# A written-out order of 6,000 steps, replaced by another, with ten steps removed, in an RWKV-7 plus SwiGLU kernel

## The chip, the cores and the metric

The program runs on one core of a Trainium2 chip. A core has a matrix engine (TensorE; its matmuls are called PE in the profile, its weight loads PEld), a vector engine (VectorE, DVE), an activation engine (ScalarE, ACT), a general engine (GpSimd, POOL) and a sync engine (SyncE, SP) that only issues DMA transfers. Matmuls read SBUF and write PSUM; the other engines move results from PSUM to SBUF. Each engine takes its instructions in the order in which the program lists them and waits on semaphores for the other engines.

The metric is the device time of one execution in microseconds, less is better. The median of several executions is compared.

## The reference

Inputs have batch 4, heads 8, sequence 768, head size 40 for the recurrent part; the feed-forward part has 3072 tokens of width 320 and 1536 hidden units. Everything is float32 on the chip; the feed-forward weights arrive as 64-bit floats. Cut to what is computed:

```python
for t in range(S):                        # per batch and head
    y[:, :, t] = einsum('bhd,bhde->bhe', r_t, state)
    Sa = einsum('bhde,bhe->bhd', state, a_t)
    state = state * w_t - outer(Sa, b_t) + outer(v_t, k_t)

x = y.transpose(0, 2, 1, 3).reshape(B * S, H * D)
xn = x / sqrt(mean(x * x) + 1e-6) * rms_g
g = xn @ w_gate
out = (g * sigmoid(g) * (xn @ w_val)) @ w_out
```

The state that stands after the last token is not an output, and the state before the first token is zero.

## The kernel before

**Chunks.** The 768 tokens are cut into 24 chunks of 32. For each chunk there are three stages. `front(c)` loads w, a, k, b and v, transposes them (helper `turned`), forms Gram matrices of k, b and a in levels of 1, 2, 4, 8 and 16 tokens with the decays between them, and writes the 32x32 triangular matrices `LT` to DRAM (`sB`) and back in another layout (`M`). `inverse(c)` inverts these matrices with some 60 small DVE operations and takes the result to DRAM (`sY`) and back into `LT`. `main(c)` multiplies the carried state `ST` by the decayed a (`aP`, kind "state"), adds the local part and solves with `LT` (kind "lower"), puts the solution into `VU`, updates the state (kind "update"), forms the scores with r, sums the levels into `y`, normalises, and leaves transposed rows in `xg`. Chunks 0 to 4 (`BLOCKED`) solve in two blocks, with two solves and a correction between them.

**Feed-forward.** `feed(g)` takes the rows of two chunks (one in the first and the last group; 13 groups) through the 12 slices of the hidden units: kinds "h64" and "hh" for gate and value, Silu on ACT, a product on DVE (`hT`), and "out" into the PSUM tile `po`. `narrow(f, h)` turns the 64-bit weights into 32-bit floats, 24 times five DVE operations and two on ACT, and it all falls into the lead of the program, since group 0 needs all 12 slices.

**The order.** Nothing is issued while these functions run. Each operation becomes a `Piece` with its engine, its needs and its issue function: 6003 in all, of which PE has 1093 (a piece is a group of matmuls, 2 to 64 instructions), DVE 2746, ACT 1092, SP 548 and POOL 524. `Plan.issue` (line 341) then issues them in the order that the text `ORDER` (line 33) writes out: each word is an offset, counted from the first piece that has not yet been issued. So ORDER sets the order on every engine and every DMA queue. `PAIRS` (line 238) gives for each use of a PSUM room (497) which of three PSUM pairs it takes. Semaphores come from the data: an order can't change a result, only the waits.

**What sets when a buffer is free.** `wan` (w and a, later r of a chunk pair) has one buffer, `M` and `Yi` one, `VU`, `LT`, `K`, `ST` and `KN` two.

**Lines that the change touches.** In `front`, line 779 on: per level `K1` is K decayed once more (DVE, and an ACT copy of the other half), `ends` (lines 789 to 798) make the next A, which at level 16 is `aP`, line 799 makes the next product of decays, `Tl[2 * l]`; line 808 on transposes the last K into `KN[32]`. In `main`, line 861: `Sdec`, the decayed state; line 881: the update and the new state.

- `aP` is read in `main` by the kind "state" alone, which runs for c > 0.
- `KN[32]` is read by the kind "update" alone.
- `Tl[32]` is read by `Sdec` alone.

The loop that calls all this goes over c from -2 to 23: `main(c)`, `feed` where a group ends, then `front(c + 2)` and `inverse(c + 2)`.

Of the kernel before, what the change touches and what calls it, by code (L numbers as in the profile page):

```python
# [16 lines left out]
P = 128  # L17
# [16 lines left out]
76 70 3 72 73 2 4 204 697 196 46 36 5 6 25 0 0 58 59 60 199 40 0 53 55 56 340 51 52 40 60 61 67 0 41 73 72 62 363  # L34
190 82 83 199 193 200 46 362 188 383 0 41 0 0 4 45 17 14 16 15 81 371 379 0 0 0 17 18 59 69 47 177 0 18 13 386 364
23 176 60 385 365 679 89 0 355 356 65 357 68 189 177 67 77 80 93 0 80 361 103 4 0 1 21 25 89 74 99 113 101 22 373
374 356 2 90 4 357 0 0 10 366 367 660 169 661 53 3 56 55 84 344 86 361 345 377 62 66 378 350 351 362 71 96 95 363
352 107 370 371 70 364 74 73 67 15 45 44 46 372 353 68 82 81 69 78 98 83 93 92 79 97 89 90 354 63 94 100 101 109 105
80 110 104 112 111 114 171 91 103 653 373 115 355 113 178 179 180 9 160 117 119 118 20 365 356 374 185 379 106 102
22 375 116 389 182 183 186 192 380 381 376 397 196 191 193 197 195 181 208 187 188 382 120 387 407 406 54 293 198  # L40
386 121 194 204 388 122 123 209 124 207 125 167 202 126 127 189 128 203 129 292 130 206 190 131 383 199 215 132 213
133 214 134 384 135 205 219 136 24 409 408 0 173 162 394 214 133 381 424 425 213 134 196 206 208 222 135 207 217 136
395 396 397 137 218 228 138 139 140 227 229 160 226 386 141 142 290 644 216 648 172 143 144 145 146 148 655 398 406
219 387 388 399 389 400 147 231 390 220 401 391 232 230 445 233 407 392 408 409 646 426 427 410 180 428 411 221 293
412 149 444 236 237 429 275 291 645 434 197 647 653 14 663 292 238 239 430 240 433 435 446 276 241 242 243 431 447
153 448 244 223 245 104 246 432 247 225 152 150 668 669 151 277 248 436 437 278 279 438 439 249 449 250 251 450 252
280 281 451 454 455 453 253 456 457 458 254 452 255 440 256 441 257 258 475 476 459 442 259 460 496 285 282 284 495
260 443 486 261 461 262 485 477 283 234 235 294 286 295 654 662 652 650 263 484 478 479 462 264 212 224 265 487 463
287 266 268 269 497 480 498 298 267 306 305 315 303 307 316 299 300 499 767 670 304 302 301 504 505 507 506 481 488
500 308 311 270 0 311 500 677 308 488 273 312 650 489 14 839 823 0 231 46 2 1 0 195 18 22 196 23 186 24 25 469 470  # L50
472 368 197 26 187 251 540 207 371 370 212 198 231 369 381 473 383 375 385 388 376 474 526 525 213 214 27 28 399 386
215 475 476 430 230 398 29 387 410 216 384 217 397 30 396 477 479 481 478 31 480 395 406 530 533 538 539 536 537 250
241 232 218 377 392 378 233 393 394 234 379 484 32 485 252 235 242 240 239 380 389 391 529 527 409 405 408 390 400
407 253 254 364 543 0 0 370 371 203 210 204 368 378 222 384 379 387 389 390 388 393 391 394 392 385 211 205 229 381
212 223 382 380 369 213 455 459 458 383 228 214 224 466 469 516 457 456 215 465 460 462 463 461 468 216 470 225 249
471 464 467 472 398 399 400 401 402 476 403 517 474 0 2 385 403 404 472 476 405 406 407 477 408 409 0 0 395 327 328
396 329 330 331 332 311 312 418 164 428 431 430 429 435 333 334 391 143 142 436 335 336 337 338 339 340 341 545 544
365 415 248 342 343 345 346 344 347 348 349 442 417 446 437 366 397 546 549 548 547 441 529 443 166 167 448 447 438
445 444 439 452 440 456 458 350 351 454 453 457 455 530 449 465 451 414 459 468 464 463 450 146 460 461 469 471 472
482 480 462 467 532 533 434 147 148 470 466 483 481 486 487 168 663 473 149 674 150 151 425 478 534 476 169 152 485  # L60
477 484 474 490 424 535 536 537 170 171 538 539 479 172 173 540 531 475 541 491 492 493 494 495 496 497 498 499 500
369 370 542 676 664 675 681 662 670 665 667 677 671 673 666 543 550 678 551 501 502 503 504 505 506 507 508 509 672
398 399 400 510 680 401 686 511 512 513 687 402 554 555 556 783 185 174 176 514 515 516 517 518 519 520 175 558 177
178 557 523 522 521 524 562 560 563 179 180 564 559 561 181 182 566 565 568 183 184 573 569 567 570 571 525 528 403
527 575 572 574 576 784 577 578 786 186 187 188 579 842 843 841 526 854 580 488 489 682 840 685 844 683 785 189 744
787 788 789 669 697 684 851 839 790 404 581 702 405 407 696 406 190 191 688 192 689 690 847 582 695 700 712 710 713
698 699 724 733 701 791 795 709 711 793 792 583 794 691 798 584 585 721 692 707 693 708 552 694 703 720 732 799 706
719 717 195 194 193 196 197 718 722 723 553 704 714 715 725 729 726 731 705 730 727 716 802 807 728 804 803 736 806
810 813 815 816 805 811 809 198 199 200 0 0 4 6 806 810 815 816 812 584 817 732 733 735 738 820 818 821 5 739 737
736 743 744 745 746 747 1 0 0 737 738 745 746 4 0 0 701 702 773 703 704 628 799 801 797 798 806 617 705 706 774 707  # L70
708 770 775 709 776 777 808 810 952 802 953 811 807 710 814 1078 1075 1082 1073 809 823 1083 711 1085 1072 1074 828
0 0 1087 5 813 0 3 5 0 0 811 4 707 708 822 709 807 808 46 47 48 53 821 816 710 817 819 711 830 52 54 49 712 820 713
0 829 840 0 781 783 782 664 5 665 0 665 790 761 666 762 776 667 670 669 778 777 763 764 773 792 791 789 787 46 0 47
42 43 770 769 44 49 788 783 48 50 45 89 797 663 666 779 781 794 90 780 684 790 791 799 800 798 0 0 0 642 652 710 594
701 384 386 387 1 576 0 10 17 6 785 0 1 650 0 380 700 8 10 573 697 927 638 922 9 2 4 712 11 5 0 698 571 12 14 779
780 782 15 591 592 796 0 792 794 702 700 703 701 568 778 0 0 0 767 768 781 365 769 770 772 773 771 367 366 695 696
697 698 699 700 701 702 703 704 706 705 708 709 710 711 712 713 714 715 716 717 718 719 720 721 722 723 724 725 726
727 728 729 730 0 1 773 782 706 730 602 603 604 605 894 783 370 731 732 733 734 735 736 367 606 372 371 368 373 797
800 799 737 738 739 786 792 740 741 787 788 918 919 905 742 743 744 904 2 789 791 745 369 374 790 793 796 746 798
794 805 795 806 801 912 747 802 748 895 803 804 807 808 809 810 1109 811 914 812 749 1098 1097 0 1102 913 747 748  # L80
912 1093 1104 926 931 749 751 750 752 0 542 546 547 570 558 0 5 0 5 314 550 551 553 554 315 9 0 565 5 6 0 0 552 543
544 561 545 576 558 559 562 564 546 376 378 377 555 557 560 575 574 556 569 570 572 227 573 571 13 595 582 7 12 9 8
10 14 15 566 567 577 578 579 730 568 394 580 585 0 0 0 212 214 213 1 215 379 649 388 389 417 572 570 571 574 575 573
576 418 419 420 524 567 565 421 2 4 580 581 363 585 582 583 587 584 589 586 3 647 648 8 5 591 588 590 593 594 712
505 703 650 592 595 596 597 598 599 600 601 602 364 651 655 653 708 707 704 718 654 7 0 0 0 0 641 647 1 566 592 593
594 595 596 597 598 599 600 601 648 651 657 567 602 656 603 604 605 652 658 606 662 664 665 607 2 7 8 653 4 654 608
655 661 699 504 659 609 660 610 666 611 667 612 9 10 663 668 669 671 670 613 672 614 673 674 615 675 616 676 3 5 617
618 0 671 682 962 487 702 704 6 706 8 613 614 842 0 7 400 698 702 711 610 611 612 613 614 704 615 616 700 617 619
712 705 706 710 715 725 716 618 620 714 959 713 960 958 969 727 723 717 726 707 728 724 9 721 736 708 967 970 838
492 722 709 718 738 737 720 733 719 732 0 6 0 0 0 4 615 617 616 618 728 628 629 723 724 734 735 745 742 743 744 747  # L90
749 729 733 737 748 540 739 746 725 678 688 689 822 395 396 398 397 0 733 731 828 830 747 682 955 829 394 815 816
# [314 lines left out]
def kernel(  # L406
# [41 lines left out]
    N = 8  # L448
# [256 lines left out]
    def front(c):  # L705
# [59 lines left out]
        for j, l in list(enumerate(LEVELS))[2:]:  # L765
# [11 lines left out]

            t = Tl[l].rearrange("p n (g x) -> p n g x", x=2)
            K1 = K_.next()
            if G == 1:  # L780
                tt(K1[:, :, :, 0:16], K[:, :, :, 0:16], t[:, :, None, :, 1].to_broadcast((P, NI, 2, 16)), MUL)
            else:
                for x in range(2):
# [316 lines left out]
```

## Time and profile before

| what | value |
|---|---|
| executions | 1035.87, 1037.38, 1040.97 us |
| median of the three | 1037.38 us |
| the profiled execution, its own time | 1039.87 us |
| its span, first to last instruction | 1038.0 us |
| mean granted TensorE clock in it | 0.952 of full |
| first feed matmul starts, last one ends | 182.8, 1032.8 us |
| feed groups 1 to 10, one each | 69 to 79 us |

The profile gives, for one execution, the busy time of each engine, the same in 40 equal slices, the clock that TensorE was granted (in tenths), the chain of waits that ended last, and groups of equal instructions with their total and mean duration. Busy time on PE is a union over overlapping matmuls: a matmul's own duration (some 200 ns for the small ones) is longer than its share of PE, since many small ones run side by side on parts of the array. Where a PE step is priced below, the time from its first matmul's start to the next step's first start is taken, from the timeline.

### The profile page before, as it was taken

How to read it: one execution, taken by the hardware profiler on the slowest of the kernel's cores; microseconds unless marked ns; L12 is line 12 of the kernel's file. 1: busy time of each engine (PE TensorE's matmuls, PEld its weight loads, DVE VectorE, ACT ScalarE, POOL GpSimd, SP SyncE). 2: the span in 40 equal slices, each digit the busy share in tenths (PEclk: the TensorE clock that was granted, in tenths of full speed). 3: DMA queues.
4: the chain of work that ended last, by engine and by line, in shares of the span. 5: the costliest groups of instructions: out<-in, count | busy, mean ns of one | idle time of the engine just before them, and what ended most of it. 6: DMA issues, size and time to landing. Idle time of an engine off the chain costs nothing.

```text
span 1038.0 us, 55525 instructions
## 1 busy us (share of the span) xinstructions
PE 934.5 (90%) x24592; PEld 760.3 (73%) x24592; DVE 790.2 (76%) x2747; ACT 498.4 (48%) x1113; POOL 306.6 (30%) x530
## 2 busy tenths in 40 slices
PE   2546767999999999999999999999999999999998
PEld 2445756877777878777778777777787787788777
DVE  8989978867869778868778679678697787777531
ACT  5566556453454464464454544534534635436131
POOL 9523234221432242233331324123232413400000
PEclk9957667899999999999999999999999999999999
DMA  7675443222242242232231232232322422420100
GB/s 159 145 173 120 99 93 82 56 63 54 43 84 38 47 95 43 60 79 42 59 84 28 62 75 55 55 68 36 76 45 55 81 41 65 75 44 8 43 7 21
DMA packets 147056, 68.89 MB, mean 66 GB/s; under 512 B 121088, under 2 KB 136384, under 8 KB 146816
## 3 DMA queue, kind: packets, MB, share of 16 engines
q1 hardware_dynamic: 128448, 42.37, 18.4%
q0 software_dynamic: 16192, 22.64, 11.8%
q8 instruction: 193, 3.16, 1.3%
q10 hardware_dynamic: 2176, 0.33, 0.2%
q14 instruction: 47, 0.39, 0.1%
HBM read 55.05 MB, written 10.22 MB: 63 GB/s over the span
## 4 chain that ended last, share of the span: by engine, by line
PE 70%; DVE 9%; DMA 7%; SPq 4%; issue 4%; ACT 2%; DVEq 0%; ACTq 0%
PE ps L532 50%; PE po L532 14%; PE ps L535 6%; SPq L529 4%; DVE Yi L486 2%; DMA LT<-sY 2%; DMA sY<-Yi 2%; DVE tmp L486 1%; DMA sB<-LT 1%; DVE LT L486 1%; DVE wf L486 1%; DMA M<-sB 1%; DVE K L486 1%; DVE y L486 1%; DVE As L486 0%
## 5 line engine op out<-in xcount | busy, mean ns | idle before, releaser
L532 PE MATMUL ps<-xg,wf 128*128 128x256 f32 (+3 forms) x1872 | 361.1, 375 | 1.1 <-DVE hT L486 0.9
L532 PEld LDWEIGHTS ps<-xg,wf 128*128 128x128 f32 (+1 forms) x1872 | 267.7, 190 | 49.1 <-issue 13.2
L532 PE MATMUL po<-wf,hT 128*128 128x320 f32 x576 | 179.7, 446 | 1.1 <-issue 1.1
L486 DVE TENSOR_TENSOR hT<-ps,sg 128x256 f32<-128x256 f32 (+1 forms) x156 | 59.8, 398 | 94.1 <-PE ps L532 56.0
L532 PEld LDWEIGHTS po<-wf,hT 128*128 128x128 f32 x576 | 102.9, 189 | 38.6 <-issue 4.0
L486 DVE TENSOR_TENSOR tmp<-Yi,M 128x24 f32<-128x24 f32 (+21 forms) x512 | 106.6, 208 | 17.4 <-DMA M<-sB 4.5
L486 DVE TENSOR_TENSOR Yi<-Yi,tmp 128x24 f32<-128x24 f32 (+21 forms) x512 | 106.8, 209 | 10.6
L509 ACT ACTIVATE sg<-ps 128x256 f32<-128x256 f32 (+1 forms) x156 | 54.0, 369 | 109.8 <-PE ps L532 106.8
L529 POOL DMA_DIRECT2D VU<-in_v_dram x92 | 53.9, 587 | 155.4 <-PE ps L532 134.4
L486 DVE TENSOR_TENSOR K<-K,T 128x512 f32<-128x512 f32 (+1 forms) x192 | 93.2, 501 | 4.4 <-PE ps L532 1.9
L519 POOL TENSOR_TENSOR ss<-ss,mhalf 128x1 f32<-128x1 f32 x24 | 14.3, 596 | 255.1 <-DVE ss L486 255.0
L532 PE MATMUL ps<-Ab,K 64*60 64x56 f32 (+2 forms) x4608 | 76.3, 220 | 12.7 <-issue 2.4
L532 PEld LDWEIGHTS ps<-Ab,K 64*60 64x60 f32 (+2 forms) x4608 | 69.3, 132 | 22.4 <-issue 10.1
L513 ACT COPY KN<-ps 128x640 f32<-128x640 f32 x96 | 65.8, 692 | 38.8 <-DVE LT L486 24.4
L529 POOL DMA_DIRECT2D kbn<-in_k_dram x92 | 54.1, 589 | 98.5 <-PE ps L532 98.5
L486 DVE TENSOR_TENSOR As<-ps,msi 128x256 f32<-128x256 f32 (+1 forms) x168 | 70.9, 453 | 15.5 <-PE ps L532 10.9
L529 POOL DMA_DIRECT2D kbn<-in_b_dram x92 | 54.1, 589 | 82.9 <-PE ps L532 81.3
L532 PEld LDWEIGHTS ps<-As,KN 128*40 128x40 f32 x3072 | 67.3, 128 | 11.6 <-issue 4.1
L532 PE MATMUL ps<-As,KN 128*40 128x32 f32 x3072 | 72.6, 208 | 2.4 <-DVE As L486 1.2
L513 ACT COPY K<-K 128x512 f32<-128x512 f32 x96 | 61.0, 636 | 27.1 <-PE ps L532 11.8
L486 DVE SCALAR_TENSOR_TENSOR Yi<-M,Yi 128x31 f32<-128x31 f32 (+6 forms) x228 | 44.5, 243 | 36.7 <-DMA M<-sB 20.0
L529 POOL DMA_DIRECT2D wn<-in_w_dram x92 | 51.8, 565 | 43.7 <-DVE KN L486 43.5
(131 smaller groups left out, 1503.4 us busy)
## 6 DMA issues: line engine op xcount, KB each, us to landing
M<-sB SPq DMA_DIRECT2D x96, 128.0 KB, 3.0
wan<-in_r_dram SPq DMA_DIRECT2D x24, 160.0 KB, 4.0
kbn<-in_k_dram POOLq DMA_DIRECT2D x92, 40.0 KB, 2.6
kbn<-in_b_dram POOLq DMA_DIRECT2D x92, 40.0 KB, 2.9
VU<-in_v_dram POOLq DMA_DIRECT2D x92, 40.0 KB, 2.7
wan<-in_w_dram POOLq DMA_DIRECT2D x46, 80.0 KB, 3.2
wan<-in_a_dram POOLq DMA_DIRECT2D x46, 80.0 KB, 2.8
wn<-in_w_dram POOLq DMA_DIRECT2D x92, 40.0 KB, 2.8
```

The lines of the kernel that those rows point to most:

```text
L486: plan.add("DVE", time + more + each * size(o), 0.087, lambda at: [fn(at(o), *m(at))], [o], aps(*args))
L509: scalar(o, [a], lambda at: nc.scalar.activation(at(o), at(a), f, **kw), aps(acc), 0.1 if f in (AF.Square, AF.Relu) else 0.0)
L513: scalar(o, [a], lambda at: nc.scalar.copy(at(o), at(a)), extra=more)
L519: plan.add("POOL", 0.5, 0.06, lambda at: nc.gpsimd.tensor_tensor(o, a, b, op), [o], [a, b])
L529: plan.add(by, 0.6 if by == "POOL" else 0.45, 0.0, lambda at: queue.dma_start(out=o, in_=i), [o], [i], load=load, since=since)
L532: return o, lhsT, rhs, lambda at: nc.tensor.matmul(at(o), lhsT, rhs, start=start, stop=stop, skip_group_check=True), 4
L535: return o, i, ident, lambda at: nc.tensor.transpose(at(o), i, ident), 2
```

## The change

Two things are done. ORDER and PAIRS are written anew: another order of the same steps, less ten. And ten steps are gone: for the last chunk (23) the decayed K at level 16 (a DVE operation and an ACT copy), `Tl[32]`, the transposes into `KN[32]` and their copy, `Sdec` and the update; for the first chunk (0) `aP` (a DVE operation and an ACT copy) and `Tl[32]`. The number of steps falls from 6003 to 5993 and that of PSUM rooms from 497 to 495. No constant, buffer or instruction of the remaining steps is changed. All lines of ORDER and PAIRS are replaced; a few are shown.

```diff
--- before.py
+++ after.py
 ORDER = """
-76 70 3 72 73 2 4 204 697 196 46 36 5 6 25 0 0 58 59 60 199 40 0 53 55 56 340 51 52 40 60 61 67 0 41 73 72 62 363
-190 82 83 199 193 200 46 362 188 383 0 41 0 0 4 45 17 14 16 15 81 371 379 0 0 0 17 18 59 69 47 177 0 18 13 386 364
...
+86 83 81 0 0 53 0 1 44 0 64 0 65 76 196 199 45 0 0 38 0 52 0 57 0 5 0 0 51 0 36 0 43 47 57 69 353 354 355 70 72 76
+78 362 0 173 186 8 75 89 371 57 81 58 56 189 94 59 82 0 0 90 58 360 352 353 2 370 371 103 0 181 19 184 90 3 113 378
...
 """
 
 PAIRS = """
-01201210121021200021102212200010110200100201020112101002120121012212012212110202010010102012120120012002120020000011
...
+01201022101021010120102221102210012100101011200212202001210220201002022222210211010102211001002121002012011110021101
...
 """
...
@@ -776,14 +776,18 @@
             copy(z["KN"][l].rearrange("p (n o e) -> p n o e", n=N, o=2), gr.rearrange("p o n t -> p n o t")[:, :, :, 16:16 + D])
 
             t = Tl[l].rearrange("p n (g x) -> p n g x", x=2)
-            K1 = K_.next()
-            if G == 1:
-                tt(K1[:, :, :, 0:16], K[:, :, :, 0:16], t[:, :, None, :, 1].to_broadcast((P, NI, 2, 16)), MUL)
-            else:
-                for x in range(2):
-                    tt(side(K1[:, :, x], l, 0), side(K[:, :, x], l, 0), t[:, :, :, 1, None].to_broadcast((P, NI, G, l)), MUL)
-            kn_ = lambda k: k.rearrange("p n x (g h l) -> p (n x) g h l", h=2, l=l)[:, :, :, 1]
-            copy(kn_(K1), kn_(K))
+            if G > 1 or c + 1 < NCH:
+                K1 = K_.next()
+                if G == 1:
+                    tt(K1[:, :, :, 0:16], K[:, :, :, 0:16], t[:, :, None, :, 1].to_broadcast((P, NI, 2, 16)), MUL)
+                else:
+                    for x in range(2):
+                        tt(side(K1[:, :, x], l, 0), side(K[:, :, x], l, 0), t[:, :, :, 1, None].to_broadcast((P, NI, G, l)), MUL)
+                kn_ = lambda k: k.rearrange("p n x (g h l) -> p (n x) g h l", h=2, l=l)[:, :, :, 1]
+                copy(kn_(K1), kn_(K))
+            if l == 16 and c == 0:
+                K = K1
+                break
             if l == 16:
                 A1, A0 = aP_.next(), A[:, :, 0:C]
                 ends = [(side(A1, l, 1), side(A1, l, 0), side(A0, l, 1), side(A0, l, 0), t[:, :, :, 0, None].to_broadcast((P, NI, G, l)))]
@@ -796,7 +800,8 @@
             for r1, l1, r0, l0, w_ in ends:
                 tt(r1, r0, w_, MUL)
                 copy(l1, l0)
-            tt(Tl[2 * l], t[:, :, :, 0], t[:, :, :, 1], MUL)
+            if G > 1 or c + 1 < NCH:
+                tt(Tl[2 * l], t[:, :, :, 0], t[:, :, :, 1], MUL)
             K, A = K1, A1
 
         sB = sB_.next()
@@ -805,9 +810,10 @@
         z["M"] = M = M_.next()
         for m in range(4):
             dma(M[m * BH:(m + 1) * BH].rearrange("p b x -> p (b x)")[:, 0:C * C], sB, "M")
-        z["KN"][32] = KN_[32].next()
-        copy(z["KN"][32].rearrange("p (n o e) -> p n o e", n=N, o=2),
-             turned(K.rearrange("p (n i) x s -> p n (i x s)", i=2), ins=TOP, outs=P)[:, :, :, 0:D])
+        if c + 1 < NCH:
+            z["KN"][32] = KN_[32].next()
+            copy(z["KN"][32].rearrange("p (n o e) -> p n o e", n=N, o=2),
+                 turned(K.rearrange("p (n i) x s -> p n (i x s)", i=2), ins=TOP, outs=P)[:, :, :, 0:D])
         z["aP"] = A
 
     def inverse(c):
@@ -859,7 +865,7 @@
         pe("lower", [mm(X[other(i, n), o, col(n % 4)], LT[own(i, n), o * N + slot(n)], VU[own(i, n), n, o, 0:D], c == 0 and n % 4 == 0, n % 4 == 3)
                     for n, i, o in by_q])
         Sdec = Sdec_.next()
-        if c > 0:
+        if 0 < c < NCH - 1:
             tt(Sdec, ST.rearrange("p n i d -> p (n i) d")[:, :, 0:D], z["T"][32].to_broadcast((P, NI, D)), MUL)
         Xs = Xs_.next()
         scale(Xs, X[:, :, 0:4 * D], -1.0)
@@ -878,14 +884,15 @@
         for i, q in each_iq:
             copy(VU[other(i, 4 * q), 4 * q:4 * q + 4, :, 0:D].rearrange("p n o d -> p o n d"),
                              U[other(i, 4 * q), :, 0:4 * D].rearrange("p o (n d) -> p o n d", n=4), more=0.09)
-        up = plan.room()
-        pe("update", [mm(up[part(o), i, col(slot(n))], kn(z, 32, i, n, o), VU[half(i), n, o, 0:D]) for n, i, o in each])
-        if c == 0:
-            copy(ST_.next()[:, :, :, 0:D].rearrange("p n i d -> p i n d"), up[:, :, 0:N * D].rearrange("p i (n d) -> p i n d", n=N))
-        elif c + 1 < NCH:
-            tt(ST_.next()[:, :, :, 0:D].rearrange("p n i d -> p i n d"),
-               up[:, :, 0:N * D].rearrange("p i (n d) -> p i n d", n=N),
-               Sdec.rearrange("p (n i) d -> p i n d", n=N), ADD)
+        if c + 1 < NCH:
+            up = plan.room()
+            pe("update", [mm(up[part(o), i, col(slot(n))], kn(z, 32, i, n, o), VU[half(i), n, o, 0:D]) for n, i, o in each])
+            if c == 0:
+                copy(ST_.next()[:, :, :, 0:D].rearrange("p n i d -> p i n d"), up[:, :, 0:N * D].rearrange("p i (n d) -> p i n d", n=N))
+            else:
+                tt(ST_.next()[:, :, :, 0:D].rearrange("p n i d -> p i n d"),
+                   up[:, :, 0:N * D].rearrange("p i (n d) -> p i n d", n=N),
+                   Sdec.rearrange("p (n i) d -> p i n d", n=N), ADD)
         if c % 2 == 0:
             tk = slice(c * C, (c + 2) * C)
             t = rn.next()
```

## What the change does to the time: a forecast

> **What bounds the kernel now.** I read the page's first two parts, then a table of five stretches, then the chain of waits, then groups kept apart by shape, for the prices.
>
> ```profile
> span 1038.0 us, 55525 instructions
> PE 934.5 (90%) x24592; PEld 760.3 (73%) x24592; DVE 790.2 (76%) x2747; ACT 498.4 (48%) x1113; POOL 306.6 (30%) x530
> ...
> PE   2546767999999999999999999999999999999998
> DVE  8989978867869778868778679678697787777531
> PEclk9957667899999999999999999999999999999999
> ```
>
> PE is full from the eighth slice (26 us each) to the end. Before that DVE is the full engine and the granted clock is low. The stretches say it in microseconds:
>
> ```profile
> core 0: us, PE busy (x) PEld busy (x) DVE busy (x) ACT busy (x) POOL busy (x), PEclk, DMA share, GB/s
> 0.00:47.00 47.00, 19.06 (x588) 17.18 (x592) 43.13 (x123) 24.76 (x46) 34.87 (x68) 1.00 0.69 152
> 47.00:187.00 140.00, 92.00 (x3493) 82.33 (x3483) 119.47 (x354) 86.97 (x176) 46.09 (x77) 0.65 0.50 114
> 187.00:222.00 35.00, 33.94 (x952) 29.07 (x948) 27.55 (x104) 15.51 (x37) 8.58 (x15) 1.00 0.29 58
> 222.00:1008.00 786.00, 763.74 (x19354) 610.75 (x19341) 596.47 (x2155) 365.05 (x835) 216.54 (x369) 1.00 0.27 55
> ```
>
> Up to 47 us DVE is busy 92% (43.13 of 47). From 47 to 187 it is busy 85%, at a clock of 0.65, so 20.5 us of it are idle. From 222 us PE is busy 97% at full clock. So the time is a DVE-bound lead of some 190 us plus the PE work left then. The chain agrees: 70% PE, 9% DVE, 7% DMA. A sum over the timeline (first feed matmul starts at 182.8 us, the last ends at 1032.8) leaves 5 us at the end, for the copy and store of the last rows.
>
> **Part 1: the removed work.** These groups give the prices:
>
> ```profile
> L535 PE MATMUL ps<-ident,K 40*128 40x40 f32 x384 | 17.4, 239 | 1.8 <-DVE y L486 0.9 <-DVE hT L486 0.8
> L532 PE MATMUL ps<-VU,KN 64*40 64x40 f32 x1536 | 22.7, 212 | 4.7 <-issue 4.4 <-ACT VU L513 0.3
> ...
> L486 DVE TENSOR_TENSOR K<-K,T 128x512 f32<-128x512 f32 x48 | 32.9, 686 | 1.8 <-ACT K L513 0.8 <-ACT T L513 0.7
> L486 DVE TENSOR_TENSOR Sdec<-ST,T 128x640 f32<-128x640 f32 x23 | 18.8, 818 | 0.2
> ...
> L486 DVE TENSOR_TENSOR aP<-Ab,T 128x256 f32<-128x256 f32 x24 | 10.0, 417 | 0.0
> ...
> L486 DVE TENSOR_TENSOR T<-T 128x16 f32<-128x16 f32 x24 | 4.0, 168 | 0.1
> ```
>
> Last chunk. The 16 transposes of K run at 969 us, where PE is full; from their start to the next step's takes 0.52 us at the median, so -0.5. The 64-instruction update runs at 1032.90, behind the last feed matmul, beside the copy and store that end the program: 0 (0.83 us if it stood earlier). DVE loses 0.69 (K), 0.17 (T) and 0.82 (Sdec), ACT the copies K (0.62) and KN (0.70). All lie at 956 to 971 us beside a full PE, and DVE waits on PE in that stretch: 0; without that cover 1.7.
>
> First chunk. DVE loses aP 0.42 and T 0.17, in the lead, where DVE is the bound: -0.6. ACT's copy of aP (0.39 at 21 us) hides behind DVE: 0. **Part 1: -1.1.**
>
> **Part 2: the new order.** Each word of ORDER is a place counted from the first step not yet issued, so both lists can be read off as steps and compared. They are near neighbours. Of the 1091 PE steps in both, half move by at most one place and nine in ten by at most 4; DVE, ACT and SP at most 7, 6 and 7; POOL, which issues most loads, 16. Every DMA is still issued, on the queue it had. One is moved past others: the first half of chunk 0's r load now stands on SP ahead of the four sB stores of chunk 0, which wait behind it until chunk 1's w and a are transposed (28.4 us; sB went at 29.0). Price 0.45 (one issue) to 4.0 (its landing); I take it inside the lead's bounds below.
>
> **Changes of array shape.** In the timeline from 225 us a full 128-row feed step of four matmuls takes 0.863 us, start to start, before another of its shape, and 0.957 before a step of another shape; for the output steps it is 1.076 and 1.170. So a change costs 0.094. From the first feed step on the old list has 480 changes, the new 477: **-0.3.**
>
> **Work ahead.** For each PE step I add the DVE work listed before it (each operation by the median of its group's start-to-start spacing, or its duration) and the PE work from it to the end (median spacing by kind). The largest sum over all steps is what the two engines need between them: 965.1 before, 963.4 after, so -1.7. Of this, 0.8 is the update that costs nothing and 1.1 is part 1, so the order adds **+0.2.** At the first feed step the sum falls from 964.2 to 961.6: 155.1 us of DVE work stand ahead of it before, 151.5 after, while the PE work done by then falls only from 64.1 to 61.8.
>
> **The lead's idle time.** These 73 us between 965 and 1038 are idle time that no list shows. The largest piece is DVE's in the lead:
>
> ```profile
> 130.00:156.00 26.00, 16.45 (x676) 14.68 (x680) 19.56 (x66) 14.74 (x30) 8.29 (x14) 0.68 0.42 93
> 156.00:182.00 26.00, 19.02 (x819) 17.06 (x815) 20.52 (x53) 16.02 (x37) 11.81 (x20) 0.76 0.39 80
> ```
>
> 11.9 us in these two slices (52 less 40.1). There chunks 2 and 3 pass through their inverse, and its result goes from SBUF to DRAM (sY) and back (LT) before PE can solve. The DVE work put between the inverse's last operation and that solve grows from 9.0 to 13.4 us for chunk 2 and from 10.0 to 12.7 for chunk 3; the way took 10.5 and 11.6 in the trace. So 7.1 us more of DVE work fills stretches in which it idled. Bounds: 0 (the idle comes back one wait later) and -11.9 (all of it gone). PE at half clock, which nothing here removes, ends a good part of it, so I take half of the 7.1: **-3.5.**
>
> **The same way late.** In the steady part the cover is PE work. From the inverse's end to the solve it falls for chunk 22 from 16.8 to 10.3 us, for 23 from 14.0 to 11.7, for 16 from 11.4 to 10.5. The way alone took 9.8 us for chunk 0 (55.48, its first sY issue, to 65.27) and 12.0 for chunk 1 (78.41 to 90.40). Bounds: -2.4 (all that PE waited for LT from 225 us on) and +8.7 (third rival). Nearest the old trace, where such covers passed without a wait, I take **+1.0.**
>
> **Sum:** -1.1 - 0.3 + 0.2 - 3.5 + 1.0 = -3.7, made against the profiled 1039.87 (span 1038.0). Off the median 1037.38, 2.5 below it, it gives **1033.7**.
>
> **Rivals.**
>
> *The clock opens earlier.* In the lead PE's steps take about double: the 64 solves of a chunk 1.33 us at 67 us against 0.79 at 993 us. The PE links of the chain between 60 and 180 us come to 13.0 us (1.41, 1.33, 1.33, 1.13, 1.38, 0.35, 1.20, 0.96, 0.34, 1.18, 1.15, 1.22). If the new order keeps PE dense enough for the full clock there, 41% of that goes (0.54 of 1.33): -5.3 more, 1028.4, and down to 1024 if most of the DVE idle goes too. For: the lists differ most in the lead. Against: PE has the same work there, and DVE still sets its pace. The Trainium skill ("TensorE: Matmul & The Clock Gate", Part 1: The HAM clock gate) has half clock as the default, lifted after a busy window of about 3.4 us and lost after an idle one, with nothing between. The trace agrees in part: the slice from 52 to 78 us shows 0.50; the 1.00 of the first 43 us does not fit its matmuls (ps<-A,K 313 ns there, 221 from 225 us on), which the page's default would explain. By that page this rival would be the outcome if the gaps shrink below a window.
>
> *Nothing but the removed work shows.* DVE's filled idle comes back at the next wait, the late covers hold: -1.2, 1036.2. For: PE steps barely move. Against: 2.6 us less stand before the first feed step.
>
> *Slower: the solve of chunk 22 waits.* PE takes its steps in order, so a late LT stops all feed work behind it. In the old run chunk 22's cover of 16.8 us took 13.0, so the inverse ended 3.8 late against the list. With 10.3 us of cover, such lateness and a way of 12.0, PE stands 12.0 + 3.8 - 10.3 = 5.5 us; chunk 23 adds the 2.3 its cover shrinks by, chunk 16 0.9: 8.7 together. It decides once the inverse runs over 0.5 us late with the short way of 9.8. With no gain in the lead the sum is -1.2 + 8.7 = +7.5: 1044.9.
>
> **How the numbers follow.** Forecast 0.42 (own range 1030 to 1037), clock 0.26, nothing 0.10, slower 0.22. About 0.5%, 5.2 us, is what a measurement tells from no change. Below 1032.2 lie nearly all of the clock case and a third of the forecast: 0.40. Above 1042.6 lie some three quarters of the slower case: 0.17. The rest is 0.43. The range 1024 to 1044.5 leaves out half of the slower case and the low edge of the clock case, 0.16 together.
>
> **What would show it.** Right: the first feed matmul at 178 to 181 us instead of 182.8, DVE idle from 130 to 182 us down to about 8, PE from 222 us on still 97% busy, no transposes of K for the last chunk. The clock case: under 70 us at half clock between 47 and 187 instead of the 98 that 0.65 of 140 us means. Slower: PE waits over 2 us on LT near 920 to 1000 us. I am wrong if the lead keeps its length and the difference sits in the steady part, where my two lists look alike.

## The result and the profile after

The changed kernel is slower: a median of 1041.89 us over 20 executions (1036.55 to 1048.76) against 1036.65 over 20 of the kernel before (1030.49 to 1045.42). The ratio is 1.0046, with an interval of 1.0026 to 1.0067, so some 5 us were lost where 3.7 were expected to be won. That is just under the 0.5% named as the bound, but with 20 executions of each the interval leaves out 1. The profiled execution took 1046.2 us, 4.3 above its median; its mean granted clock was 0.939, before 0.952.

The page of the changed kernel, its first two parts and the row of the DMA queue that carries instructions:

```profile
span 1044.4 us, 55364 instructions
...
PE 940.6 (90%) x24512; PEld 763.5 (73%) x24512; DVE 790.8 (76%) x2742; ACT 495.9 (47%) x1110; POOL 309.6 (30%) x530
...
PE   2557667999998999999999989999999999999998
...
DVE  9999978786967778769678676798697687776531
...
PEclk9656758999999999999999999999999999999999
...
q8 instruction: 192, 3.15, 1.3%
```

From the eighth slice on, the part that was full before, nothing is new in PE's row but two eights, in the 13th slice (313 to 339 us) and in the 24th (600 to 627 us). The same stretches as those shown of the kernel before, of the changed kernel (columns as there):

```profile
core 0: us, PE busy (x) PEld busy (x) DVE busy (x) ACT busy (x) POOL busy (x), PEclk, DMA share, GB/s
0.00:47.00 47.00, 20.47 (x608) 18.17 (x608) 43.18 (x120) 25.49 (x47) 40.26 (x75) 0.84 0.67 156
47.00:187.00 140.00, 95.38 (x3584) 86.31 (x3586) 124.71 (x371) 87.40 (x176) 41.32 (x71) 0.66 0.48 113
187.00:222.00 35.00, 34.19 (x937) 28.47 (x932) 27.95 (x111) 17.40 (x43) 11.15 (x19) 1.00 0.34 67
222.00:1008.00 786.00, 759.41 (x19032) 605.17 (x19031) 585.32 (x2114) 358.76 (x822) 216.29 (x365) 0.99 0.27 55
```

From 47 to 187 us DVE does 124.71 us of work instead of 119.47: the lead is tighter, as forecast. From 222 to 1008 us PE does 759.41 instead of 763.74 and 322 matmuls fewer (19032 against 19354), at a clock of 0.99 instead of 1.00. So the lead won and the steady part lost. The places on the timeline say how much. The first feed matmul starts at 174.7 us (before 182.9), group 2 of the feed-forward at 290.9 (297.1), and from there to the end of the last output matmul, which I call **the rest** from here on, it takes 749.0 us instead of 735.9. Until group 2 it is 6.2 ahead; it gives back 13.1.

What PE waited for from 225 to 1010 us, first in the kernel before, then in the changed one (engine, tile and line, what was waited for: us in total, times, longest us):

```profile
PE ps L532 <- issue: 12.2, 16, 1.8
PE ps L532 <- DMA LT<-sY: 2.4, 3, 1.3
...
PE ps L535 <- issue: 1.5, 1, 1.5
PE po L532 <- issue: 1.1, 1, 1.1
```

```profile
PE ps L532 <- issue: 19.2, 17, 2.8
PE ps L535 <- issue: 2.6, 3, 1.4
PE po L532 <- issue: 1.5, 2, 1.1
```

The waits for LT, the subject of the slower rival, are gone. What grew is "issue", time in which PE waited for nothing that the profile shows: from 14.8 us (12.2 + 1.5 + 1.1) to 23.3. The largest of these, in PE's timeline of the changed kernel (start, us, engine, line, operation, tiles, count, idle time before it):

```profile
332.66 0.78 PE L532 MATMUL ps<-ST,aP 64*32 64x40 f32 x64
333.38 0.69 PE L532 MATMUL ps<-VU,LT 32*32 32x40 f32 x53
336.83 0.47 PE L532 MATMUL ps<-VU,LT 32*32 32x40 f32 x11 [2.76 <-issue]
337.23 4.63 PE L532 MATMUL po<-wf,hT 128*128 128x320 f32 x8
```

The solve of chunk 7 is a step of 64 small matmuls with one wait at its head. PE runs 53 of them, stands for 2.76 us, and runs the other 11. The profile shows no semaphore between the 53rd matmul and the 54th. What else went on there, in the table of stretches of the changed kernel (columns as above):

```profile
322.00:334.00 12.00, 11.93 (x386) 9.07 (x378) 9.23 (x23) 5.53 (x13) 4.67 (x9) 1.00 0.35 61
334.00:337.00 3.00, 0.24 (x17) 0.17 (x10) 0.12 (x1) 0.00 (x0) 2.21 (x4) 0.82 1.00 209
337.00:343.00 6.00, 6.00 (x37) 3.84 (x34) 0.75 (x3) 1.02 (x4) 0.00 (x0) 0.52 0.21 40
343.00:350.00 7.00, 7.00 (x123) 5.41 (x120) 5.51 (x28) 4.74 (x14) 0.56 (x1) 1.00 0.01 4
```

Up to 334 us PE is at work for 11.93 of 12 us, with 386 matmuls at full clock. Then the DMA engines are full (share 1.00, 209 GB/s) while PE, DVE and ACT all stand. After that comes a stretch at a clock of 0.52, in which 6 us hold 37 matmuls. The 8 output matmuls that stand in it take 4.63 us, where such a step of 8 takes 2.35 at full clock (at 389 us in the kernel before). So the stop cost 2.76 us, and the half clock behind it (6.8 us long) cost some 3.4 more if it loses half of its length.

**A place in the instruction stream.** I counted PE's instructions in order of their start, weight loads, matmuls and semaphore instructions together, and noted each stop of PE over 0.7 us from 205 us on by that count, modulo 256 (193 or 194, since a semaphore instruction can stand in between):

```
kernel    stops over 0.7 us at place 193 modulo 256                 elsewhere
before    9, at 254 266 295 419 489 532 585 614 626 us              5
changed   17, at 214 248 259 289 337 380 396 423 465 495 507        2
          580 591 605 622 635 744 us
```

Instructions come in blocks: queue q8 moves 3.15 MB in 192 packets, 16.4 KB each. PE has 49,297 instructions by my count, which is 192.6 times 256, and 16.4 KB (16,384 bytes) over 256 is 64 bytes; the kernel before has 49,460 (193.2 times 256) and 193 packets. So the stops stand where one block of PE's program ends. The Trainium skill ("Runtime: NRT & Kernel Launch", Instruction fetch mechanics) has instructions refilled in 16 KiB blocks of 256, and the cost of crossing such a boundary as "mostly hidden". The trace agrees with the block, and differs on the cost: of 150 boundaries between 225 and 1000 us in the kernel before, 16 stop PE for more than 0.3 us, 14.4 us together; in the changed kernel it is 22 of 147, 23.3 us. All of the "issue" time from 225 to 1010 us stands at such boundaries, in these two profiles as in all that follow. The packets tie it to the fetching of instructions: in all 17 profiles, PE goes on 1.2 to 1.65 us after the packet has landed that brings the next block, at each of the 284 stops over 0.3 us.

### The profile page after: what moved, and what is told of

The parts are those of the page before. It is cut to its first block, busy times and chain, and to the rows that moved or that the text cites. A ratio compares the mean times of both kernels' runs of the same rounds, so it can differ in the third digit from the quotient of the medians.

```text
span 1044.4 us, 55364 instructions
## 1 busy us (share of the span) xinstructions
PE 940.6 (90%) x24512; PEld 763.5 (73%) x24512; DVE 790.8 (76%) x2742; ACT 495.9 (47%) x1110; POOL 309.6 (30%) x530
## 3 DMA queue, kind: packets, MB, share of 16 engines
q0 software_dynamic: 16192, 22.64, 11.4%
q8 instruction: 192, 3.15, 1.3%
## 4 chain that ended last, share of the span: by engine, by line
PE 71%; DVE 13%; DMA 5%; issue 4%; ACT 3%; SPq 3%; DVEq 0%; ACTq 0%
PE ps L532 50%; PE po L532 15%; PE ps L535 6%; SPq L529 3%; DVE Yi L486 2%; DVE tmp L486 2%; DVE y L486 1%; DVE As L486 1%; DMA wf<-in_moe_w_out_dram 1%; DMA M<-sB 1%; DVE K L486 1%; DVE LT L486 1%; DMA sB<-LT 1%; DVE wf L486 1%; DVE Ab L486 1%
## 5 line engine op out<-in xcount | busy, mean ns | idle before, releaser
L532 PEld LDWEIGHTS ps<-xg,wf 128*128 128x128 f32 (+1 forms) x1872 | 269.0, 191 | 53.0 <-issue 13.3
L532 PE MATMUL po<-wf,hT 128*128 128x320 f32 x576 | 182.3, 451 | 1.8 <-issue 1.5
L486 DVE TENSOR_TENSOR K<-K,T 128x256 f32<-128x256 f32 (+1 forms) x191 | 91.5, 495 | 1.7 <-ACT sg L509 0.5
L532 PE MATMUL ps<-Ab,K 64*60 64x56 f32 (+2 forms) x4608 | 79.6, 225 | 13.6 <-ACT K L513 3.6
L532 PEld LDWEIGHTS ps<-Ab,K 64*60 64x60 f32 (+2 forms) x4608 | 72.6, 137 | 23.7 <-issue 10.4
L513 ACT COPY K<-K 128x512 f32<-128x512 f32 x95 | 60.3, 635 | 27.0 <-DVE K L486 13.3
L519 POOL TENSOR_TENSOR ss<-ss,mhalf 128x1 f32<-128x1 f32 x24 | 16.7, 698 | 183.7 <-DVE ss L486 174.2
```

The source lines that it names most:

```text
L486: plan.add("DVE", time + more + each * size(o), 0.087, lambda at: [fn(at(o), *m(at))], [o], aps(*args))
L513: scalar(o, [a], lambda at: nc.scalar.copy(at(o), at(a)), extra=more)
L519: plan.add("POOL", 0.5, 0.06, lambda at: nc.gpsimd.tensor_tensor(o, a, b, op), [o], [a, b])
L532: return o, lhsT, rhs, lambda at: nc.tensor.matmul(at(o), lhsT, rhs, start=start, stop=stop, skip_group_check=True), 4
```

## The experiments

Two theories at first: the loss lies in the new order of the rest; or it lies in the lead, or in the ten steps that are gone, and only shows later. Then, once the stops were seen, two more: the loss is a matter of where the blocks happen to be cut; or the new rest is slower at whatever cut. "Order of before" below always means less the ten steps. The rest and the stops ("issue" waits of PE from 225 to 1010 us) are from the one profiled execution of each run; ratios are to the kernel before on the same chip. There were four chips (e1 to e4, e5 to e8, e9 to e11, e12 to e15), on which the kernel before had medians of 1037.76, 1033.68, 1034.89 and 1035.19 us, so microseconds of different groups are comparable to some 4 us only.

### Which part (e1 to e4)

e1 is the changed kernel with the order of before; e2 has the new order for its first 1717 steps (up to some 281 us), then the old one; e3 the reverse, the old order up to step 1717, then the new one. e4 is the changed kernel once more. PAIRS goes with each part, so the choice of PSUM pairs is not parted from the order. The edit of e2 against e1 (e3 has the first line of e1 and the last ones of the changed kernel):

```diff
 ORDER = """
-76 70 3 72 73 2 4 201 694 193 46 36 5 6 25 0 0 58 59 60 196 40 0 53 55 56 337 51 52 40 60 61 67 0 41 73 72 62 360
+86 83 81 0 0 53 0 1 44 0 64 0 65 76 196 199 45 0 0 38 0 52 0 57 0 5 0 0 51 0 36 0 43 47 57 69 353 354 355 70 72 76
...
 101 108 103 107 109 99 100 104 105 110 114 115 111 116 2 0 0 0 1 0 0 0
 """
```

> The order of before, with the ten steps left out and nothing else moved. Theory A (the removed work is worth what the rows say, 1.1 us, and the order does all the rest): ratio to before 0.997 to 1.001. Theory B (leaving steps out disturbs the old order, for instance the first chunk's lead): ratio over 1.002.

> The new order up to its step 1717 of 5993 (in its profile about 281 us), then the remaining steps in the order of before; the ten steps are out. Theory A (the new lead gains the 6 us by which the changed kernel's second feed group begins early, and the new steady part loses more than that): faster, ratio 0.993 to 0.997. Theory B (the early start is a matter of one profile, the lead gains nothing in the median): ratio 0.998 to 1.002. Theory C (the loss comes from the lead in most executions): ratio over 1.003.

> The order of before up to step 1717 (about 287 us), then the remaining steps in the new order; the ten steps are out. Theory A: slower than the changed kernel, by the 11 to 13 us that its steady part lost against before: ratio 1.008 to 1.012, with PE standing in the middle of its groups and the clock at half in at least one stretch after 330 us. Theory B: ratio 1.003 to 1.006, as the changed kernel. Theory C: ratio 0.998 to 1.002.

> The changed kernel once more, for a second profile. Theory A with losses that sit at fixed places of the new order: ratio 1.003 to 1.007, PE standing again near 334, 422 and 620 us, the clock at half for 10 us or more after 222 us. If the places change from execution to execution: as slow, but other places. Theory B: the lead's gain of 6 us is not there the second time.

| kernel | median us | ratio to before | feed 2 starts | the rest | stops |
|---|---|---|---|---|---|
| e1, old order | 1036.07 | 0.9977 (0.995 to 1.0003) | 294.9 | 733.2 | 14.4 |
| e2, new lead | 1034.0 | 0.9958 (0.9934 to 0.9983) | 292.1 | 732.6 | 13.3 |
| e3, new rest | 1044.82 | 1.0067 (1.0041 to 1.0092) | 294.3 | 743.2 | 19.1 |
| e4, changed again | 1042.14 | 1.0032 (1.0005 to 1.006) | 295.6 | 742.9 | 22.4 |

Both kernels with the new rest are slower than before, both with the old rest are not. e3 lies between the forecasts of its two theories (1.008 to 1.012 and 1.003 to 1.006), so the loss was milder there than theory A had it. The new lead alone with the old rest beats both kernels of this study. So the loss is in the order of the rest, with its PAIRS, and neither in the lead nor in the removed steps. The waits of PE from 225 to 1010 us in e2:

```profile
PE ps L536 <- issue: 11.6, 14, 1.4
...
PE po L536 <- issue: 1.0, 1, 1.0
PE ps L539 <- issue: 0.7, 2, 0.4
```

And e4 stops in the solve of chunk 7 just as the first profile did, on its timeline:

```profile
337.54 0.69 PE L532 MATMUL ps<-VU,LT 32*32 32x40 f32 x53
340.96 0.33 PE L532 MATMUL ps<-VU,LT 32*32 32x40 f32 x11 [2.73 <-issue]
```

After 53 of 64 matmuls again, 2.73 us, 4 us later on the clock: the place belongs to the program, not to the moment. That execution has one stretch of half clock behind it, 3.4 us (0.51 in the table of stretches from 341.3 to 344.8 us) and the only one of its rest, where 10 or more were expected and the first profile had 6.8 there and 17.0 in all of the rest. How much of it comes differs between executions of one kernel.

### Where the blocks are cut (e5 to e8)

A few small matmuls more, at the very start, shift every later instruction against the blocks, and change no order. Each "-" adds one matmul of 64 rows and 32 columns, which is four PE instructions, into columns of `po` that nothing reads. e5 has 8 of them in the changed kernel (a shift of 32), e6 32 (128); e7 has 32 (128) and e8 56 (224) in the kernel of e2.

```diff
-    plan.warm = lambda: nc.tensor.matmul(po_[:, 0, DM:DM + P], ident, ident, start=False, stop=False, skip_group_check=True)
+    plan.warm = lambda: nc.tensor.matmul(po_[0:64, 0, DM:DM + 32], ident[0:64, 0:64], ident[0:64, 0:32], start=False, stop=False, skip_group_check=True)
...
-179 171 180 0 351 18 15 72 99 98 352 97 107 96 44 369 370 43 353 48 659 323 0 71 72 81 14 17
+179 171 180 0 351 18 15 72 99 98 352 97 107 96 44 369 370 43 353 48 659 323 0 71 - - - - - - - - 72 81 14 17
```

> The changed kernel with 8 small extra matmuls (64x64 by 32 columns, written to columns of po that nothing reads; 32 PE instructions) behind the second transposing step, where PE idles. They move every later PE instruction by 32 places against the blocks of 256 in which PE's instruction stream seems to arrive. Theory A (PE's stops in the steady part are waits for the next block of its instruction stream, and their length depends on how fast the block before was used up): the stops move to other instructions, still one place in 256, and, where blocks are cut now, more of them are short: 5 to 13 us slower than the changed kernel (ratio to before 1.008 to 1.016), stops from 225 us on of 26 to 36 us in sum instead of 22. Theory B (the stops are made by bursts of data transfers at fixed times of the order): same places in time, the same sum within 3 us, ratio 1.002 to 1.007.

> As the run before, with 32 extra matmuls (128 instructions, half a block). Theory A: other places again (the stop near 334 us in the solve of chunk 7 goes), but by the block lengths about the same sum, 20 to 28 us, and a ratio of 1.001 to 1.009. Theory B: the same places, the stop near 334 us stays.

> The kernel with the new lead and the old rest, with 32 extra matmuls (128 instructions). Theory A: its blocks are cut best there: stops 3 to 7 us less than without the shift (13.6 us), ratio to before 0.989 to 0.994, which would be below both kernels. Theory B: as without, 0.994 to 0.998.

> The same with 56 extra matmuls (224 instructions). Theory A: its blocks are cut worst there: stops 5 to 10 us more than 13.6, ratio 1.000 to 1.006. Theory B: as without the shift, 0.994 to 0.998.

Measured: e5 1045.6 us, 1.0109 (1.0079 to 1.0139); e6 1046.62, 1.0129 (1.0099 to 1.0159); e7 1030.4, 0.9968 (0.9946 to 0.9989); e8 1047.76, 1.0123 (1.009 to 1.0155). The solve of chunk 7 in e5, on PE's timeline:

```profile
336.92 0.78 PE L536 MATMUL ps<-ST,aP 64*32 64x40 f32 x64
337.64 0.55 PE L536 MATMUL ps<-VU,LT 32*32 32x40 f32 x37
338.89 0.47 PE L536 MATMUL ps<-VU,LT 32*32 32x40 f32 x27 [0.71 <-issue]
```

With 32 instructions more ahead, that is 16 loads and 16 matmuls, the stop comes after 37 matmuls instead of 53, and 37 is 53 less 16. In all of these kernels most stops still stand at place 193 or 194 of 256, now in other steps. This shows that it is the block and not the step at which PE stops. It did not help: the stop shrank here to 0.71 us, and others came elsewhere. One of 2.1 us, ending at 628 us in e5, is again a block's end; the longest of e5 is not, but a wait for DVE at place 249:

```profile
598.60 3.59 PE L536 MATMUL ps<-As,KN 128*40 128x32 f32 x109 [2.93 <-DVE y L490]
```

**What the stops do not explain.** The place of the stops was foreseen, their sums and the times mostly were not. e5 has 13.2 us of stops (15.3 with the one at 628, which the profile puts down to a load) where 26 to 36 were expected, e6 16.6 (20 to 28), e8 17.1 (18.6 to 23.6), and e6 and e8 are slower than forecast all the same. e7 has 9.3 us, 4 less than e2 as expected, and is no faster against before than e2 is. So the sum of the stops does not follow the time from cut to cut. The profiles of e5 and e6 are of executions 3.9 and 2.8 us below their medians, so they may not show what makes the others slow; that is open. And the cut alone moves the old rest from 0.9968 (e7) to 1.0123 (e8), 1.5% with no word of the order changed.

### Fewer fast blocks by hand (e9 to e11)

If a stop comes from a block that is used up quickly, exchanging neighbouring PE steps, a small one against a large one, should spread the small ones. I chose such exchanges by an estimate of each block's duration from the steps' median spacing: 12 exchanges in the changed kernel (e9), 16 in that of e2 (e10), 8 in that of e7 (e11). One of those of e9:

```diff
-431 418 1160 1147 1144 1161 1151 821 822 1092
+431 821 418 1160 1147 1144 1161 1151 822 1092
```

> The changed kernel with 12 exchanges of neighbouring PE steps behind its first lead (a group of many small matmuls changes places with a feed step or another small group beside it), chosen so that fewer blocks of 256 PE instructions are used up in under 3.45 us; nothing else. Theory A (stops are waits for the instruction stream): their sum falls by about 5 us by the block lengths (26.6 to 21.7 worked out, 24.4 measured before), and the time by 3 to 9 us, ratio to before 0.995 to 1.002. Theory B (the stops come from something else): the time stays, 1.003 to 1.007.

> The kernel of the new lead and the old rest, with 16 such exchanges. Theory A: stops 6 us less than its 17.5, ratio 0.989 to 0.994. Theory B: 0.994 to 0.998.

> The kernel of the new lead and the old rest, with 32 extra matmuls and 8 such exchanges. Theory A: a little below the same without exchanges (0.9968), whose blocks leave 1.6 us to gain: 0.991 to 0.996. Theory B: as that one, 0.995 to 0.999.

e9 took 1040.34 us, 1.0053 (1.0033 to 1.0074), e10 1038.65, 1.0033 (1.0007 to 1.0058), e11 1032.96, 0.9979 (0.9952 to 1.0006). e9 and e10 are misses: the first stayed where the changed kernel was, the second became slower than e2, and e11 can't be told from e7. In e9 the stops fell to 16.3 us (from 23.3 and 22.4), yet the rest took 741.6. In e10 they fell to 11.4 us, and the rest took 738.5 against 732.6. So stops are not all there is to it. The profile of e10 shows where it went: PE's waits for the other engines and for LT from 225 to 1010 us grew from 5.0 us in e2 to 8.7 (2.5 of them one wait for DVE's hT, ending at 747 us), and its rest has 6.8 us at half clock, where e2 has none. In e9 such waits grew to 6.4 us, from 2.4 and 3.1. So an exchange costs waits that my spacing doesn't show.

### New rest against old rest at four cuts (e12 to e15)

To part the cut from the order, both rests were run at shifts of 64 and 192 as well (16 and 48 words "-"), beside those of 0 and 128.

> The changed kernel with 16 extra matmuls (64 instructions) in the lead. Theory A1 (the old and the new steady part differ only in how their instruction stream happens to be cut into blocks): over the cuts tried, the new order ranges as widely as the old one and some cut brings it to the time of before or below, ratio 0.995 to 1.002 here or at 192. Theory A2 (the new steady part is slower at any cut): 1.004 or more here and at 192.

> The changed kernel with 48 extra matmuls (192 instructions). A1: as for 64. A2: 1.004 or more.

> The kernel of the new lead and the old rest, with 16 extra matmuls (64 instructions). A1: its cuts, too, spread from 0.996 to 1.012, here by the block lengths near the unshifted one: 0.994 to 1.002. A2: 0.994 to 1.000.

> The same with 48 extra matmuls (192 instructions), by the block lengths one of the two worst cuts. A1 and the theory of the instruction stream: 1.004 to 1.012. If cuts do not matter: 0.994 to 0.998.

| shift | new rest: ratio | its rest, stops, half clock (us) | old rest: ratio | its rest, stops, half clock (us) |
|---|---|---|---|---|
| 0 | 1.0046, e4 1.0032 | 749.0, 23.3, 17.0; e4 742.9, 22.4, 3.4 | e2 0.9958 (0.9934 to 0.9983) | 732.6, 13.3, 0 |
| 64 | e12 1.0173 (1.0145 to 1.02) | 748.8, 17.2, 10.2 | e14 1.0011 (0.9985 to 1.0037) | 735.6, 12.8, 0 |
| 128 | e6 1.0129 (1.0099 to 1.0159) | 745.2, 16.6, 6.8 | e7 0.9968 (0.9946 to 0.9989) | 733.7, 9.3, 3.4 |
| 192 | e13 1.0233 (1.0201 to 1.0265) | 756.1, 27.1, 6.8 | e15 1.0131 (1.0099 to 1.0163) | 748.3, 17.8, 10.2 |

e12 and e13 came out as theory A2 had them; e14 lies just above A2's range (0.994 to 1.000), e15 just above its own (1.004 to 1.012). At each cut the new rest is slower than the old one, by 0.7 to 1.6% in time (8 to 17 us) and by 8 to 16 us in the rest, and at each it stops longer, by 4 to 10 us. The cut alone moves either kernel by 1.7 to 2%. The extra matmuls come with it: the first feed matmul starts later with them (180.9 us in e13 and 180.0 in e15, against 173.9 to 176.3 without), but group 2 does not (293.7 in e13 against 290.9 and 295.6, 291.9 in e15 against 292.1 in e2). So both are true: the time depends on the cut, and at the same cut the new order of the rest costs about 1.3% (the mean of the four differences, 0.88 or 0.74, 1.62, 1.61 and 1.02%).

The worst of them, e13, in its waits of PE from 225 to 1010 us:

```profile
PE ps L537 <- issue: 22.7, 20, 3.0
PE ps L540 <- issue: 4.4, 6, 1.6
PE ps L537 <- DMA LT<-sY: 2.2, 3, 1.5
```

27.1 us of stops, and 2.2 us of waits for LT, against 2.4 in the kernel before: the way that the slower rival spoke of is not what makes e13 slow.

## Why the prediction was wrong

**The lead's idle time (-3.5).** The mechanism held. DVE's idle time from 130 to 182 us, 11.9 before, is 8.7 in the changed kernel ("down to about 8" was the mark), 10.4 in e4 and 8.9 in e2, against 11.7 and 11.4 with the old lead (e1, e3). The two slices of the changed kernel:

```profile
130.00:156.00 26.00, 17.45 (x669) 15.84 (x659) 20.51 (x63) 14.60 (x29) 9.94 (x17) 0.59 0.43 93
156.00:182.00 26.00, 20.27 (x810) 17.99 (x807) 22.74 (x56) 18.81 (x43) 11.40 (x19) 0.82 0.40 88
```

The first feed matmul comes at 174.7, 176.3 and 173.9 us (changed, e4, e2), earlier than the 178 to 181 that were named, against 178.9 and 179.7 (e1, e3): 4.3 us earlier on the means. At group 2 the means differ by 1.7 us (292.9 against 294.6), so more than half is used up on the way. In time, e2 is 0.19% below e1, 2.0 us, less than their intervals are wide. So the sign is right, and the size is somewhere between 0 and the bound.

**The removed work (-1.1).** e1 is the kernel before without the ten steps: 0.9977, which is -2.4 us with an interval of -5.2 to +0.3. The term fits and can't be told from nothing. Of the groups named, the transposes of K went from 384 matmuls to 368 and the updates from 1536 to 1472.

**Changes of array shape (-0.3)** is below what can be measured, and no run was made for it.

**The same way late (+1.0)** was too dark, and so was the rival built on it. The covers of chunks 22, 23 and 16 did shrink in the list, and no wait for LT is left from 225 us on: 2.4 us before, none in the changed kernel. In this profile the term came out at its lower bound, -2.4; in e4, the same kernel, 1.4 us of such waits are left (one, at 794 us). The way itself was misread: no sY issue stands at 55.48 us, where the chain passes to SP's issue of a weight load. Chunk 0's four stand from 51.60 to 56.25, so its way to 65.27 us took 13.7 us from the first and 9.0 from the last; for chunk 1 (75.24 to 80.72, landing at 90.40) it was 15.2 and 9.7.

**The clock rival** did not come: 0.66 from 47 to 187 us instead of 0.65, in the changed kernel as in e1 and e2, with the old lead or the new.

**Work ahead (+0.2) is the step that failed.** It priced each PE step of the steady part at the median spacing of its kind, as if a step cost the same wherever it stands. Of the case that the text kept open one half came: the lead did not keep its length, but "the difference sits in the steady part, where my two lists look alike". Over the profiles at shift 0 the new rest takes 749.0, 742.9 and 743.2 us, the old one 735.9, 733.2 and 732.6: 11.1 us more on the means. The stops account for 7.4 of it (means 21.6 and 14.2 us; 7.6 if counted from group 2 on). Half clock accounts for some 3.4 more: stretches of 17.0, 3.4 and 3.4 us against 0, 3.4 and 0 in the rest, with half of their length lost. (Two of these, in e3 and e1, follow waits for DVE and not stops at a block's end.) This account is from one execution each and its second part scatters; at the other cuts the same sum gives 9.5 of 13.2 us, 9.0 of 11.5 and 7.6 of 7.8.

Why PE stops longer in the new order is shown in part. By the lists, more places of it would be used up quickly: from the first feed matmul on, stretches of 256 PE instructions that take under 2 us by the median spacings begin at 1618 places of the old list and at 1986 of the new one, 23% more. Such stretches are among the small matmuls (64 of them, with their loads, take half a block), and a move of "at most 4 places" for nine in ten steps, which the prediction took for nearly nothing, is enough to bring a solve beside an update or a transpose that had a feed step between them. But only one place in 256 is a boundary, and as the blocks are cut at shift 0, no more of them are used up quickly: from 225 to 1000 us, 25, 25 and 28 blocks took under 3.3 us with the old rest (before, e1, e2), and 26, 25 and 26 with the new one (changed, e4, e3).

What differs there is when the packet of the next block starts. The stops over 0.3 us whose packet started more than 1.75 us after the boundary before come to 0.9, 0 and 2.8 us with the old rest, and to 7.6, 7.1 and 3.2 with the new one: 4.8 of the 7.4 us on the means. The changed kernel has five of them, which end at 337, 396, 423, 605 and 744 us. Its table for the time from the boundary before to the start of each late packet (columns as above):

```profile
331.30:334.20 2.90, 2.70 (x146) 2.06 (x134) 2.40 (x5) 0.00 (x0) 2.90 (x6) 1.00 0.79 167
390.20:393.50 3.30, 3.30 (x60) 2.35 (x56) 3.23 (x14) 0.84 (x2) 0.00 (x0) 1.00 0.04 11
418.40:420.90 2.50, 2.50 (x72) 2.03 (x72) 1.58 (x3) 0.38 (x1) 0.61 (x2) 1.00 0.94 242
600.40:602.60 2.20, 2.20 (x71) 1.56 (x61) 1.94 (x8) 1.59 (x5) 0.00 (x0) 1.00 0.04 7
739.80:741.90 2.10, 2.10 (x44) 1.64 (x46) 2.10 (x8) 1.27 (x3) 0.00 (x0) 1.00 0.44 70
```

In two of the five the DMA engines were nearly full (0.79 and 0.94), in two they were nearly idle (0.04). So bursts of loads at a block's fetch are likely a part of the cause (the last section has their tie to late packets over all runs), but no run moved the loads alone, and what made the packets late at 393.5 and 602.6 us is open. And since e9 and e10 lowered the stops and not the time, it is argued and not shown that fewer stops would give the 11 us back.

The sign was in a row that the prediction itself showed: the update's 4.7 us of idle time before it, 4.4 of them put down to "issue". I read that as no wait at all. It is a wait for something that has no semaphore, and asking what it is would have led to the stops, though not to their price in the new order.

## What to carry to other kernels

Where a tuned kernel is full on PE with many small matmuls, "issue" time inside a step is a cost of its own: look at whether it stands at one place of the instruction count modulo 256, at how fast the block before it was used, and at when the packet of the next block started. A reordering should then be compared at several shifts of the instruction stream, since a shift alone moved these kernels by up to 2%. Moving large matmuls between the groups of small ones lowered the stops here and did not lower the time (e9, e10). A change of order is also best tried in halves: the new lead with the old rest (e2, 0.9958, and e7, 0.9968) is the version to keep here, though another shift of it (e15, 1.0131) is slower than before.

## What the runs showed of the hardware

- **A block of 256 PE instructions takes some 3.4 us to replace.** In the six kernels of shift 0, where PE stops for over 0.3 us, the packet that brings the next block starts about 0.9 us (the median; 0.7 to 1.2 by kernel) after the boundary before it, takes about 1.1 us, and PE goes on about 1.4 us after it has landed. Blocks used up in under 1.75 us are followed by 1.5 us of standing on the mean, those of 1.75 to 2.25 us by 1.0, of 2.25 to 2.75 by 0.5, of 2.75 to 3.25 by 0.3; of 647 blocks that lasted over 4 us, 6 are followed by more than 0.3 (at most 1.2).
- **The packet starts later when the DMA engines are busy.** Over all 17 profiles it starts 0.7 us (the median) after the boundary before where other queues took under a tenth of the DMA engines' time in the 1.5 us behind that boundary (1199 blocks), and 1.7 us where they took over nine tenths (94). The longest stop of the changed kernel fell together with a DMA share of 1.00 and 209 GB/s, where twelve loads that POOL had issued from 329 to 336 us and SP's transfers met; in e4 the share at the same stop was 1.05. A kernel with the same order and those loads elsewhere was not tried, so that these loads made this stop is not shown.
- **Short stops are enough to halve the clock.** All 25 stretches of half clock in the rest but one (e1, 746 us) begin within 3 us of a stop of 1.2 us or more, and last 3.4 or 6.8 us. They do so whatever PE waited for: 8 of these 24 stops are waits for DVE or for LT, away from a block's end. The Trainium skill ("TensorE: Matmul & The Clock Gate", Part 1: The HAM clock gate) has a window of about 3.4 us, half clock after an idle one and full clock after a busy one. The lengths agree with it. The stops that close the gate here are shorter than such a window (1.2 to 3.4 us), and many of that length close nothing.
- **Executions of one kernel differ by 12 to 15 us** from lowest to highest (1036.55 to 1048.76, 1030.49 to 1045.42), so a single profile can't size a difference of 0.5%; that of e12 ran 6.2 us below its median.
